# A new static order for a fused attention and mixture-of-experts kernel: due times, line counting and filler windows of its scheduler

## The chip, the core and the metric

The kernel runs on one core of a Trainium2 chip. A core has five engines, each with its own instruction stream: TensorE (PE in the profile; its weight loads are listed apart as PEld), VectorE (DVE), ScalarE (ACT), GpSimd (POOL) and SyncE (SP). Sixteen DMA engines move data between HBM and the on-chip memory, and all queues share them. The metric is the device time of one execution in microseconds. The median of the three runs of the kernel before is 178.59 us (177.97 to 179.07).

## The reference: banded attention, then soft mixture of experts

```python
# q, k, v: float32 [8 batches, 8 heads, 576 positions, 64]
scores = (q @ k.T) / sqrt(64)
# heads 0..3: position i sees i-31..i
# heads 4..7: position i sees every 4th of i-124..i
attn = softmax(where(mask[head], scores, -1e9)) @ v
x = attn.transpose(0, 2, 1, 3).reshape(4608, 512)

# phi [512, 32], w1 [8, 512, 1024], w2 [8, 1024, 512], float32
logits = x @ phi                          # [4608, 32]
d = softmax(logits, axis=0)               # over tokens
slot_input = (d.T @ x).reshape(8, 4, 512)
for e in range(8):
    slot_out[e] = relu(slot_input[e] @ w1[e]) @ w2[e]
out = softmax(logits, axis=1) @ slot_out.reshape(32, 512)   # [4608, 512]
```

The inputs are 61.9 MB in HBM, the output is 9.4 MB.

## The kernel before: units, stages, and a scheduler that writes the order

The attention is cut into eight **units**: a unit is a pair of batches and one of the two kinds of head (even units: plain band, odd units: dilated band). A unit arrives in one of three staging buffers `stg` as bf16 (the DMA converts), and goes through these stages, each a handful of PE instructions with its follow-up on another engine:

- **T** (`st_T`, four pieces; PE lines L582 for even and L577 for odd units): transposes of the staged rows into PSUM, copied into the buffer `TT` by ACT (L603). When the fourth piece has been transposed, the staging buffer is free for the load of the unit three later.
- **S** (`st_S`, six pieces; L621): scores, then exp on ACT (L628) into `PT`, then the mask on DVE (L636).
- **V** (`st_V`, four; L646): values transposed back, copied by DVE (L651) into `VN`.
- **P** (`st_P`, four; L675): probabilities times values, then a reciprocal and a product on DVE (L684, L686) into `XB`.
- **X** (`st_X`, four; L703): transposes of `XB`, copied to `XT` by DVE (L715) or ACT (L716), whichever the scheduler picks.
- **L, E, A** (`st_L`, for each batch after its odd unit; L730, L761, L774): logits and their exp, the exp transposed into `ET`, and the accumulation of slot inputs in PSUM.

After the last A come the closing stages, with due times from 1000 on: the folding of the accumulator (L861), the first expert product (L883), row sums (L930), transposes (L901), the second expert product `ffn2` (L957) as its weights arrive, then the output in two column halves for the first 1536 tokens (L1009, L1022; the factor `so_sb` of each half is made at L991) and whole for the rest (L1066). The weights `w1` go to the buffer `WD`; the last of `w2` go into `stg` (L806) and, for experts 5 to 7, into `TT` (L473), which only comes free when attention has read it.

All loads are issued by POOL in one fixed order (`load_first` L438, `load_unit` L417 and L424, `wload` L473, `wpair` L806), and each waits on POOL for its target buffer to come free. The stores are issued by SP and ACT.

No order is written by hand. Each instruction group is an `Op` with engine, cost and a **due time** (`key`). `Prog.schedule` is a greedy list scheduler that plays the program through with those costs: on each engine it looks for the earliest possible start, takes all ready groups that could start within 0.12 us of it, and places the one with the smallest due time. The order it finds is emitted as static streams with semaphores. Where the played-through PE would idle inside one of the windows of `FILL`, the scheduler inserts **fillers** (L1084): 512-column matmuls of a constant tile whose result nobody reads. Their number is fixed when the kernel is built; on the chip they are executed whether PE has the time or not.

Due times are `u * PACE + x`, with PACE = 13.1 for unit `u`, and an `x` for each stage: for example `0.5 * j` for T, `4.0 + 1.3 * i` for S, `8.5 + 2.0 * g` for P.

Of the kernel before, what the change touches and what calls it, by code (L numbers as in the profile page):

```python
# [16 lines left out]
N_SLOTS = 32  # L17
FF = 1024
SCALE = 1.0 / (D ** 0.5)
CT = 72  # L20
NU = 8
QB = 96
HALO = 32
FILL = ((1.5, 9.0, "h", 0.4, 0.43), (9.5, 13.5, "h", 0.6, 0.25), (13.5, 116.0, "h", 0.3, 0.216),
        (13.5, 24.0, "rf", 0.3, 0.216), (116.0, 143.0, "hrfc", 0.15, 0.216))


class DmaSem:
# [25 lines left out]
class Op:  # L54
    n = 0

    def __init__(self, e, fn, cost, key, mode):
        self.e, self.fn, self.cost, self.key, self.mode = e, fn, cost, key, mode
        self.deps, self.alloc, self.touch, self.sems = [], [], [], None
        self.end = self.ev = self.snap = None  # L60
        self.bytes = 0
        self.wr = []
        self.id = Op.n
        Op.n += 1
# [47 lines left out]
class Prog:  # L112
# [4 lines left out]
        self.ops = []  # L117

    def op(self, e, fn, r=(), w=(), a=(), alloc=(), cost=0.5, key=0.0, mode="f",
           sem=None, nbytes=0, after=(), ndma=1):  # L120
        o = Op(e, fn, cost, key, mode)
        deps = list(after)
        for b in r:
            deps += b.ready
        for b in w:
            b.fresh()
            deps += b.prev
        for b in a:
            deps += b.prev
        seen = set()  # L130
        for d in deps:
            if d.id not in seen:
# [12 lines left out]
        o.sems = sem  # L145
        o.bytes = nbytes
        o.ndma = ndma
        self.ops.append(o)
        return o

    def schedule(self, filler, fill_window):
# [13 lines left out]
        dma_free = 0.0  # L165
        mode = "f"
        order = []

        def place(o, t0, e):
            nonlocal dma_free, mode  # L170
            o.e = e
            cost = o.cost[e] if isinstance(o.cost, dict) else o.cost
            end = t0 + cost
            if e == "pe":
                if o.mode != mode:
                    end += 0.03
                mode = o.mode
            free[e] = end
            o.end = end
            if o.sems is not None:  # L180
                dma_free = max(dma_free, t0 + 3.2) + o.bytes / 424e3
                o.end = dma_free + 0.45
            for t in o.touch:
                t.left -= 1
                t.pool.use(t, o)
            order.append(o)

        while ready:
            picks = {}
            for o in ready:  # L190
                if o.e == "pool" and o is not pool_ops[ipool]:
                    continue
                if o.e == "sp" and o is not sp_ops[isp]:
                    continue
                got, tal, ok, taken = [], 0.0, True, {}
                for t in o.alloc:
                    f = t.pool.find(t.size, taken.get(id(t.pool), ()))
                    if f is None:
                        ok = False
                        break  # L200
                    got.append((t, f[0]))
                    tal = max(tal, f[1])
                    taken.setdefault(id(t.pool), []).extend(f[0])
                if not ok:
                    continue
                for e in (o.e if isinstance(o.e, tuple) else (o.e,)):
                    t0 = max(free[e], tal + self.LAT[e])
                    for d in o.deps:
                        t0 = max(t0, d.end + (self.LAT[d.e] if d.e != e or e != "pe" else 0.0))
                    if e == "pe" and o.mode != mode:  # L210
                        t0 += 0.08
                    picks.setdefault(e, []).append((t0, o, got))
            best = None
            for e, c in picks.items():
                lim = min(x[0] for x in c) + 0.12
                t0, o, got = min((x for x in c if x[0] <= lim), key=lambda x: (x[1].key, x[1].id))
                if best is None or t0 < best[0]:
                    best = (t0, o, got, e)
# [87 lines left out]
def bass_dilated_sliding_attn__then__soft_moe_slots_kernel(  # L306
# [93 lines left out]
    b_expT, b_expX = [Buf() for _ in range(B)], Buf()  # L400
    b_siT, b_h, b_hT, b_so = Buf(), [Buf(), Buf()], [Buf(), Buf()], [Buf(), Buf()]

    PACE = 13.1

    def due(u, x):
        return u * PACE + x

    def load_unit(u):
        bp, ty, s = u // 2, u % 2, u % 3
# [46 lines left out]
    def wload(name, parts=((0, 8, 0, 512),)):  # L456
        ap, b = HOME[name]
        e = int(name[2:])
        first_ = name[:2] == "w1"
        src = (moe_w1 if first_ else moe_w2)[e]  # L460
        c = 4 if first_ else 8
        v_ = src.rearrange("(p c) f -> p c f", c=c)
        d_ = ap.rearrange("p (c f) -> p c f", c=c)
        for lo, hi, c0, c1 in parts:
            if first_:
                dst, vs = d_, v_
            else:
                dst, vs = d_[:, lo:hi, c0:c1], v_[:, lo:hi, c0:c1]
            sem = DmaSem(nc, f"s_{name}_{len(b.parts)}")
            pb = Buf()  # L470
            for al in b.al:
                pb.prev = pb.prev + al.ready + al.reads
            o = op("pool", lambda g, dst=dst, vs=vs: [g.dma_start(dst, vs)],  # L473
                   after=pb.prev, a=[pb], cost=0.6, sem=sem,
                   nbytes=2097152 * (hi - lo) * (c1 - c0) // 4096)
            b.parts.append((lo, hi, c0, c1, pb))
            b.ready.append(o)

# [87 lines left out]
    def st_T(u, j):  # L566
# [5 lines left out]
        def pe(t):  # L572
            for a in range(2):
# [10 lines left out]
                            src[:, hx, c, :], ident[0:96, 0:96])  # L584
            return i_
        o = op("pe", pe, r=[b_id, b_stg[s] if u else b_half[j // 2]], w=[pt], alloc=[pt],
               cost=0.86 if ty == 0 else 0.75, mode="h" if ty == 0 else "f",
               key=due(u, 0.5 * j))
        if u == 0:
            b_stg[0].reads.append(o)  # L590

        def ev(ac):
# [9 lines left out]
                sv = sv.rearrange("p (s w) a k -> p s w a k", w=4)  # L602
            return ac.activation(d, sv, ACTF.Copy)  # L603
        op("act", ev, r=[pt], **{"w" if j == 0 else "a": [b_TT[u % 2]]}, cost=0.8,
           key=due(u, 0.8 + 0.5 * j))

    def bankb2(t, a):
        return psb[:, t.phys[0] + a, :]
# [1 line left out]
    def st_S(u, i):  # L610
# [4 lines left out]
        def pe(t):  # L615
# [7 lines left out]
                                  win(u, 0, h01, blk_, bpar)[64 * hx:64 * hx + 64],  # L623
                                  start=True, stop=True)
            return i_
        k0 = due(u, 4.0 + 1.3 * i)
        op("pe", pe, r=[b_TT[u % 2]], w=[sc], alloc=[sc, pt], cost=0.22, mode="r", key=k0)
        op("act", lambda ac: ac.activation(  # L628
            sbt(pt)[:, 0:768].rearrange("p (x n) -> p x n", x=2), pair(sc)[:, :, 0:384],
            ACTF.Exp, scale=SCALE), r=[sc], w=[pt], cost=0.71, key=k0 + 0.6)  # L630
# [2 lines left out]
        def mk(dv):  # L633
            m = mask[ty][:, m0:m0 + 4, :].rearrange("p m x -> p (m x)")
            p_ = sbt(pt)[:, 0:768].rearrange("p (x n) -> p x n", x=2)
            return dv.tensor_tensor(p_, p_, m.unsqueeze(1).to_broadcast([128, 2, 384]), AluOp.mult)  # L636
        op("dve", mk, r=[b_mask[ty]], w=[pt], cost=0.47, key=k0 + 1.5)

    def st_V(u, g):
        bpar, h01 = g // 2, g % 2  # L640
# [3 lines left out]
        def pe(t):  # L644
# [1 line left out]
                i_ = t.transpose(bankb(pv)[:, 128 * m:128 * m + 128],  # L646
                                 win(u, 2, h01, m, bpar), ident[:, :])
            return i_
        k0 = due(u, 4.5 + 2.0 * g)
        op("pe", pe, r=[b_id, b_TT[u % 2]], w=[pv], alloc=[pv, vn], cost=0.35, key=k0)  # L650
        op("dve", lambda dv: dv.tensor_copy(  # L651
            sbt(vn)[:, :, :, 0:64],
            bankb(pv)[:, 0:768].rearrange("p (m x d) -> p m x d", m=6, x=2)),
# [2 lines left out]
    def st_P(u, g):  # L656
# [12 lines left out]
        def pe(t):  # L669
# [6 lines left out]
                                  sbt(pts[i])[:, o_:o_ + 128],  # L676
                                  sbt(vn)[:, m, half, 0:65], start=True, stop=True)
            return i_
        k0 = due(u, 8.5 + 2.0 * g)
        op("pe", pe, r=list(pts.values()) + [vn], w=[po], alloc=al, cost=0.46, key=k0)  # L680

        def pv():
            return pair(po)[0:QB, :, 0:390].rearrange("p x (m d) -> p x m d", d=65)
# [7 lines left out]
    def st_X(u, bpar, x):  # L691
# [9 lines left out]
        def pe(t):  # L701
# [1 line left out]
                i_ = t.transpose(bankb(px)[:, QB * m:QB * m + QB],  # L703
                                 sbt(xb)[:, m, 128 * x:128 * x + 128], ident[0:QB, 0:QB])
            return i_
        k0 = due(u, 13.0 + 4.0 * bpar + 0.8 * x)
        op("pe", pe, r=[b_id, xb], w=[px], alloc=al, cost=0.31, key=k0)

        def ev(en):
            d, s_ = sbt(xt)[:, x, :], bankb(px)[:, 0:S]  # L710
# [9 lines left out]
    def st_L(b, u):  # L720
# [3 lines left out]
        def pe(t):  # L724
# [5 lines left out]
                    i_ = t.matmul(o_, phi_pad[:, c].rearrange("p j i -> p (j i)"), rhs,  # L730
                                  start=c == 0, stop=c == 3)
            return i_
        k0 = due(u, 15.5 + 4.0 * (b % 2))
        op("pe", pe, r=[x0, x1, b_phi], w=[lg], alloc=[lg], cost=1.0, key=k0)
# [4 lines left out]
        for h_ in range(2):  # L739
            def cp(dv, h_=h_):  # L740
                n = expT[:, S * b:S * b + S].rearrange("p (i y x) -> p x y i", x=2, y=2)
                return dv.tensor_copy(
                    expX[:].rearrange("p (x y i) -> p x y i", x=2, y=2)[:, :, h_],
                    n[:, :, h_, 96 * (1 - h_):96 * (1 - h_) + 48])
            op("dve", cp, r=[b_expT[b]], **{"w" if h_ == 0 else "a": [b_expX]}, cost=0.15,
               key=k0 + 2.2)
        pe_t = tile(psum, 1)
        et = tile(pET)

        def pe2(t):  # L750
# [13 lines left out]
        op("pe", pe2, r=[b_expT[b], b_expX, b_sel] + b_expT[b + 1:b + 2], w=[pe_t], alloc=[pe_t, et], cost=0.56, key=k0 + 2.4)  # L764
# [5 lines left out]
        def pe3(t):  # L770
# [8 lines left out]
        op("pe", pe3, r=[et, xb0, xb1], a=[b_acc, t_acc], cost=0.35, mode="c", key=k0 + 4.0)  # L779

    mk = sb("mk", [15, 5, 2, 4])
    turns = []
# [73 lines left out]
    for y in range(2):  # L856
        fo = tile(psum, 1)

        def pe_f(t, y=y, fo=fo):
# [4 lines left out]
        op("pe", pe_f, r=[b_psA, b_fold], w=[fo], alloc=[fo], cost=1.0, key=K1 - 0.5 + 0.1 * y)  # L864
# [214 lines left out]
    def filler(n):  # L1079
        t = tile(psum, 1)  # L1080

        def pe(te):
# [2 lines left out]
                               wrm[:].unsqueeze(1).to_broadcast([128, 4, 128]), start=True, stop=True)  # L1085
            return i_
        o = Op("pe", pe, 0.216 * n, -1, "f")
        t.left = 1
        o.touch = [t]
        o.alloc = [t]  # L1090
# [45 lines left out]
```

## Time and profile before

| | before |
|---|---|
| median of three runs | 178.59 us (177.97 to 179.07) |
| the profiled execution's own time | 177.96 us |
| its span on the core | 176.2 us |
| PE / DVE / ACT / POOL busy | 80% / 64% / 53% / 24% |
| HBM read / written | 61.93 MB / 9.44 MB |
| fillers (L1084) | 60 |

The busy shares are means over the whole span: PE's covers pipelined matmuls with modelled ends and the fillers. "DMA" in the 40 slices is the mean busy share of the 16 DMA engines in tenths, "GB/s" is what they wrote (for the loads half of what they read, since fp32 becomes bf16). The chain of waits is followed back from the last instruction, at each step to what released it. What lies around the span in the profiled execution is 177.96 - 176.2 = 1.8 us.

### The profile page before, as it was taken

Reading aid. Unit: us, or ns where it says so; the run is one execution under the profiler, and the core shown is the slowest. Engines: PE = TensorE matmul, PEld = TensorE weight load, DVE = VectorE, ACT = ScalarE, POOL = GpSimd, SP = SyncE. Lnnn points to the kernel's source line nnn. Section 1 sums busy time; section 2 is a strip of 40 time slices with the busy share of each in tenths; the row PEclk is TensorE's granted clock in tenths of the full one; section 3 lists DMA queues with packets and bytes.
Section 4 is the critical chain, followed back from the end, with each engine's and each line's share of the span. In section 5 each row is a group of like instructions: output and inputs, shape, how many; then the busy total and the mean of one; then the engine's idle time right before and its main releaser. Section 6 shows DMA issues by size and latency. Waiting matters only on the chain.

```text
span 176.2 us, 5741 instructions
## 1 busy us (share of the span) xinstructions
PE 140.8 (80%) x2573; PEld 100.2 (57%) x2574; DVE 113.5 (64%) x264; ACT 93.9 (53%) x143; POOL 42.3 (24%) x80
## 2 busy tenths in 40 slices
PE   7689988787988889797978898888999995599000
PEld 2166677566778667576956677864656643343000
DVE  6830986992897599479589489789932302379400
ACT  2044767744767875665875675774410201589300
POOL 7997105202200800500200200099900000000000
PEclk9969999999999999999999999999999999879955
DMA  4999999999999999999998999999999999999997
GB/s 70 176 238 202 197 217 210 229 230 192 215 215 212 228 230 193 216 209 217 237 219 190 216 219 214 216 214 219 214 205 206 208 194 196 305 326 398 450 424 298
DMA packets 12696, 40.80 MB, mean 232 GB/s; under 512 B 2240, under 2 KB 8896, under 8 KB 9408
## 3 DMA queue, kind: packets, MB, share of 16 engines
q0 software_dynamic: 8272, 30.94, 88.0%
q1 hardware_dynamic: 2768, 7.93, 11.4%
q10 hardware_dynamic: 1632, 1.57, 2.6%
q8 instruction: 20, 0.33, 0.7%
q14 instruction: 4, 0.03, 0.0%
HBM read 61.93 MB, written 9.44 MB: 405 GB/s over the span
## 4 chain that ended last, share of the span: by engine, by line
PE 33%; DVE 24%; DMA 18%; POOL 7%; ACT 6%; issue 4%; POOLq 0%; DVEq 0%
DMA TT<-in_moe_w_dram 15%; DVE PT L636 7%; DVE XB L686 7%; PE ps L582 7%; PE ps L577 5%; PE ps L703 4%; ACT PT L628 4%; DVE VN L651 4%; PE ps L730 4%; DVE WD L991 3%; DMA stg<-in_v_dram 3%; PE ps L646 3%; PE ps L621 3%; POOL TT L473 2%; POOL stg L806 2%
## 5 line engine op out<-in xcount | busy, mean ns | idle before, releaser
L603 ACT ACTIVATE TT<-ps 128x864 f32<-128x864 f32 x32 | 28.6, 896 | 27.6 <-PE ps L582 18.8
L628 ACT ACTIVATE PT<-ps 128x768 bf16<-128x768 f32 x48 | 36.7, 815 | 9.0 <-PE ps L621 8.9
L686 DVE TENSOR_TENSOR XB<-ps,RV 96x768 bf16<-96x768 f32 x32 | 30.3, 947 | 0.6
L651 DVE COPY VN<-ps 128x768 bf16<-128x768 bf16 x32 | 17.5, 546 | 6.3 <-PE ps L646 6.2
L1084 PE MATMUL ps<-wrm 128*128 128x512 bf16 x60 | 19.1, 446 | 1.1 <-DVE wrm L490 1.1
L675 PE MATMUL ps<-VN,PT 128*128 128x65 bf16 x384 | 17.8, 194 | 2.1 <-DVE PT L636 0.8
L582 PE MATMUL ps<-ident,stg 96*64 96x96 bf16 x576 | 16.0, 213 | 4.2 <-DMA stg<-in_v_dram 2.1
L715 DVE COPY XT<-ps 128x576 bf16<-128x576 bf16 x19 | 11.4, 598 | 10.9 <-PE ps L703 10.7
L582 PEld LDWEIGHTS ps<-ident,stg 96*64 96x64 bf16 x576 | 13.9, 114 | 7.5 <-DMA stg<-in_v_dram 2.6
L703 PE MATMUL ps<-ident,XB 96*128 96x96 bf16 x192 | 13.3, 207 | 4.9 <-DVE XB L686 3.3
L675 PEld LDWEIGHTS ps<-VN,PT 128*128 128x128 bf16 x384 | 14.5, 98 | 4.5 <-DVE PT L636 1.5
L992 ACT ACTIVATE WD<-ps,rtok 128x256 f32<-128x256 f32 (+1 forms) x22 | 10.7, 554 | 10.8 <-PE ps L1009 9.6
L646 PE MATMUL ps<-ident,TT 128*128 128x128 bf16 x192 | 16.0, 221 | 0.6 <-DVE VN L651 0.4
L621 PE MATMUL ps<-TT 64*128 64x96 bf16 x384 | 14.8, 204 | 1.2 <-ACT PT L628 1.1
L577 PE MATMUL ps<-ident,stg 96*128 96x96 bf16 x288 | 14.9, 206 | 0.3 <-DVE XB L686 0.3
L703 PEld LDWEIGHTS ps<-ident,XB 96*128 96x128 bf16 x192 | 9.6, 98 | 8.1 <-DVE XB L686 5.6
L636 DVE TENSOR_TENSOR PT<-PT,mask_d 128x768 bf16<-128x768 bf16 x24 | 12.9, 546 | 0.7 <-ACT PT L628 0.2
L577 PEld LDWEIGHTS ps<-ident,stg 96*128 96x128 bf16 x288 | 13.0, 98 | 0.4 <-DVE XB L686 0.4
L646 PEld LDWEIGHTS ps<-ident,TT 128*128 128x128 bf16 x192 | 10.8, 98 | 4.2 <-issue 1.3
L636 DVE TENSOR_TENSOR PT<-PT,mask_p 128x768 bf16<-128x768 bf16 x24 | 12.7, 539 | 0.1
L621 PEld LDWEIGHTS ps<-TT 64*128 64x128 bf16 x384 | 9.4, 94 | 5.8 <-ACT PT L628 2.5
L716 ACT ACTIVATE XT<-ps 128x576 bf16<-128x576 bf16 x13 | 8.5, 651 | 4.2 <-PE ps L703 3.9
(95 smaller groups left out, 184.1 us busy)
## 6 DMA issues: line engine op xcount, KB each, us to landing
WD<-in_moe_w_dram POOLq DMA_DIRECT2D x7, 1024.0 KB, 31.0
stg<-in_moe_w_dram POOLq DMA_DIRECT2D x5, 1024.0 KB, 25.7
stg<-in_q_dram POOLq DMA_DIRECT2D x4, 576.0 KB, 22.0
stg<-in_k_dram POOLq DMA_DIRECT2D x4, 576.0 KB, 24.0
stg<-in_v_dram POOLq DMA_DIRECT2D x4, 576.0 KB, 26.6
out_dram<-WD SPq DMA_DIRECT2D x2, 1024.0 KB, 5.3
out_dram<-WD SPq DMA_DIRECT2D x1, 2048.0 KB, 8.5
out_dram<-stg SPq DMA_DIRECT2D x1, 2048.0 KB, 10.8
```

Of the source, the lines that this page charges most:

```text
L577: i_ = t.transpose(bankb2(pt, a)[:, 96 * kk:96 * kk + 96], two[:, c, :], ident[0:96, 0:96])
L582: i_ = t.transpose(bankb2(pt, a)[64 * hx:64 * hx + 64, 96 * kk:96 * kk + 96], src[:, hx, c, :], ident[0:96, 0:96])
L603: return ac.activation(d, sv, ACTF.Copy)
L621: i_ = t.matmul(pair(sc)[:, hx, QB * x:QB * x + QB], win(u, 1, h01, blk_, bpar)[64 * hx:64 * hx + 64], win(u, 0, h01, blk_, bpar)[64 * hx: ...
L628: op("act", lambda ac: ac.activation(sbt(pt)[:, 0:768].rearrange("p (x n) -> p x n", x=2), pair(sc)[:, :, 0:384], ACTF.Exp, scale=SCALE), ...
L636: return dv.tensor_tensor(p_, p_, m.unsqueeze(1).to_broadcast([128, 2, 384]), AluOp.mult)
L646: i_ = t.transpose(bankb(pv)[:, 128 * m:128 * m + 128], win(u, 2, h01, m, bpar), ident[:, :])
L651: op("dve", lambda dv: dv.tensor_copy(sbt(vn)[:, :, :, 0:64], bankb(pv)[:, 0:768].rearrange("p (m x d) -> p m x d", m=6, x=2)), r=[pv], w= ...
L675: i_ = t.matmul(pair(po)[:, bk, 65 * po_:65 * po_ + 65], sbt(pts[i])[:, o_:o_ + 128], sbt(vn)[:, m, half, 0:65], start=True, stop=True)
L686: op("dve", lambda dv: dv.tensor_tensor(sbt(xb)[:].rearrange("p m (x h d) -> p h x m d", x=2, h=2)[:, h01], pv()[:, :, :, 0:64], sbt(rv)[: ...
L703: i_ = t.transpose(bankb(px)[:, QB * m:QB * m + QB], sbt(xb)[:, m, 128 * x:128 * x + 128], ident[0:QB, 0:QB])
L1084: i_ = te.matmul(bank(t).rearrange("p (a x) -> p a x", a=4), wrm[:], wrm[:].unsqueeze(1).to_broadcast([128, 4, 128]), start=True, stop=True)
```

## The change: other due times, a model of PE's instruction lines, a longer filler window

The diff, cut to its core:

```diff
+TOL, LINE, FETCH0 = 0.1297, 5.8, 193
+DUE = {"pace": 12.51, "T": -1.24, "Tj": 6.38, "Te": -39.52, "S": 10.02, "Si": 1.09,
+       "m": 13.16, "V": 10.46, "Vg": 5.39, "P": 9.84, "Pg": 7.23, "X": 43.57, "Xb": -45.81,
+       "L": 4.93, "Lb": -10.82, "x": 11.4}
...
-        (13.5, 24.0, "rf", 0.3, 0.216), (116.0, 143.0, "hrfc", 0.15, 0.216))
+        (13.5, 24.0, "rf", 0.3, 0.216), (116.0, 147.0, "hrfc", 0.15, 0.216))
...
+            if o.port and e in port:
+                port[e] = end
+            if e == "pe" and o.n:
+                done = 0
+                while count + o.n - done >= 256:
+                    done += 256 - count
+                    count = 0
+                    at = end - cost * (o.n - done) / o.n
+                    end += max(0.0, entry + LINE - at)
+                    entry = max(at, entry + LINE)
+                count += o.n - done
...
-                dma_free = max(dma_free, t0 + 3.2) + o.bytes / 424e3
+                dma_free = max(dma_free, t0 + 3.2) + o.bytes / 421.5e3
...
+                    if o.port and e in port:
+                        t0 = max(t0, port["pool" if e == "dve" else "dve"])
...
-                lim = min(x[0] for x in c) + 0.12
+                lim = min(x[0] for x in c) + TOL
...
-    PACE = 13.1
...
-        return u * PACE + x
+        return u * DUE["pace"] + x
...
-               key=due(u, 0.5 * j))
+               key=due(u, DUE["T"] + DUE["Tj"] * j))
...
-           key=due(u, 0.8 + 0.5 * j))
+           key=due(u, DUE["T"] + DUE["Te"] + DUE["Tj"] * j))
...
-        k0 = due(u, 8.5 + 2.0 * g)
+        k0 = due(u, DUE["P"] + DUE["Pg"] * g)
...
-        k0 = due(u, 13.0 + 4.0 * bpar + 0.8 * x)
+        k0 = due(u, DUE["X"] + DUE["Xb"] * bpar + 0.8 * x)
...
-        k0 = due(u, 15.5 + 4.0 * (b % 2))
+        k0 = due(u, DUE["L"] + DUE["Lb"] * (b % 2))
```

The scheduler's played-through PE now counts its instructions (two for each matmul). Each time the count passes 256, it enters a new line, and it may do so no earlier than 5.8 us after it entered the line before. S, V, the masks' key and the key of `expX` get new constants in the same way. The line `port` is without effect on the order: it is set for DVE groups alone, so the value that a DVE group compares with stays zero. Two costs of loads in the model change by a few per cent.

What this makes of the instruction streams: **POOL and SP keep their order, instruction for instruction**, and so do the groups of each engine after the last A, but for fillers. No DMA is added, removed or resized. Every group of the attention stays; what moves is:

- the interleaving on PE, DVE and ACT. For units 6 and 7, for example, with `T7.0` the first piece of T of unit 7 (fillers are `w`):

```
before  L4 X22 S6.0 V6.0 X23 S6.1 E4 L5 A4 V6.1 S6.2 S6.3 V6.2 E5 P6.0 S6.4 S6.5 A5
        V6.3 P6.1 P6.2 T7.0 X24 T7.1 X25 T7.2 P6.3 T7.3 X26 V7.0 S7.0 ...
after   X20 X21 V6.0 S6.0 V6.1 X22 X23 L4 S6.1 L5 E4 T7.0 P6.0 A4 E5 S6.2 S6.3 S6.4 A5
        V6.2 S6.5 P6.1 V6.3 T7.1 T7.2 P6.2 T7.3 P6.3 X24 X25 S7.0 V7.0 ...
```

- 12 of the 32 copies to `XT`, which go from DVE to ACT (19 and 13 before, 7 and 25 after);
- the fillers: 60 before, 75 after. Ahead of the first S 26 in both; from there to the last A 25 before and 9 after; behind the last A 9 before and 40 after:

```
before  A7 w*4 fold F1 row sums transposes w*5  ffn2*64                  half 0 ffn2*14 half 1 rest
after   A7 w*4 fold F1 row sums transposes w*11 ffn2*32 w*19 ffn2*24 w*2 ffn2*4 w*4 ffn2*4
        half 0 ffn2*14 half 1 rest
```

More of the change, by code (lines that the diff above doesn't have):

```diff
@@ L61, in __init__ @@
         self.bytes = 0
+        self.n = 0
+        self.port = False
         self.wr = []
@@ L119, in op @@
     def op(self, e, fn, r=(), w=(), a=(), alloc=(), cost=0.5, key=0.0, mode="f",
-           sem=None, nbytes=0, after=(), ndma=1):
+           sem=None, nbytes=0, after=(), ndma=1, n=0, port=False):
         o = Op(e, fn, cost, key, mode)
@@ L147, in op @@
         o.ndma = ndma
+        o.n = 2 * n
+        o.port = port
         self.ops.append(o)
@@ L167, in schedule @@
         order = []
+        count, entry = 256 - FETCH0, -LINE
+        port = {"dve": 0.0, "pool": 0.0}
         def place(o, t0, e):
-            nonlocal dma_free, mode
+            nonlocal dma_free, mode, count, entry
             o.e = e
@@ L474, in wload @@
                    after=pb.prev, a=[pb], cost=0.6, sem=sem,
-                   nbytes=2097152 * (hi - lo) * (c1 - c0) // 4096)
+                   nbytes=2097152 * (hi - lo) * (c1 - c0) * (108 if c1 - c0 < 512 else 100) // 409600)
             b.parts.append((lo, hi, c0, c1, pb))
@@ L586, in st_T @@
         o = op("pe", pe, r=[b_id, b_stg[s] if u else b_half[j // 2]], w=[pt], alloc=[pt],
-               cost=0.86 if ty == 0 else 0.75, mode="h" if ty == 0 else "f",
-               key=due(u, 0.5 * j))
+               cost=0.86 if ty == 0 else 0.75, mode="h" if ty == 0 else "f", n=18 if ty else 36,
+               key=due(u, DUE["T"] + DUE["Tj"] * j))
         if u == 0:
@@ L625, in pe @@
             return i_
-        k0 = due(u, 4.0 + 1.3 * i)
-        op("pe", pe, r=[b_TT[u % 2]], w=[sc], alloc=[sc, pt], cost=0.22, mode="r", key=k0)
+        k0 = due(u, DUE["S"] + DUE["Si"] * i)
+        op("pe", pe, r=[b_TT[u % 2]], w=[sc], alloc=[sc, pt], cost=0.22, mode="r", n=8, key=k0)
         op("act", lambda ac: ac.activation(
@@ L636, in mk @@
             return dv.tensor_tensor(p_, p_, m.unsqueeze(1).to_broadcast([128, 2, 384]), AluOp.mult)
-        op("dve", mk, r=[b_mask[ty]], w=[pt], cost=0.47, key=k0 + 1.5)
+        op("dve", mk, r=[b_mask[ty]], w=[pt], cost=0.47, key=k0 + DUE["m"], port=True)
     def st_V(u, g):
@@ L648, in pe @@
             return i_
-        k0 = due(u, 4.5 + 2.0 * g)
-        op("pe", pe, r=[b_id, b_TT[u % 2]], w=[pv], alloc=[pv, vn], cost=0.35, key=k0)
+        k0 = due(u, DUE["V"] + DUE["Vg"] * g)
+        op("pe", pe, r=[b_id, b_TT[u % 2]], w=[pv], alloc=[pv, vn], cost=0.35, n=6, key=k0)
         op("dve", lambda dv: dv.tensor_copy(
@@ L678, in pe @@
             return i_
-        k0 = due(u, 8.5 + 2.0 * g)
-        op("pe", pe, r=list(pts.values()) + [vn], w=[po], alloc=al, cost=0.46, key=k0)
+        k0 = due(u, DUE["P"] + DUE["Pg"] * g)
+        op("pe", pe, r=list(pts.values()) + [vn], w=[po], alloc=al, cost=0.46, n=12, key=k0)
         def pv():
@@ L705, in pe @@
             return i_
-        k0 = due(u, 13.0 + 4.0 * bpar + 0.8 * x)
-        op("pe", pe, r=[b_id, xb], w=[px], alloc=al, cost=0.31, key=k0)
+        k0 = due(u, DUE["X"] + DUE["Xb"] * bpar + 0.8 * x)
+        op("pe", pe, r=[b_id, xb], w=[px], alloc=al, cost=0.31, n=6, key=k0)
         def ev(en):
@@ L732, in pe @@
             return i_
-        k0 = due(u, 15.5 + 4.0 * (b % 2))
-        op("pe", pe, r=[x0, x1, b_phi], w=[lg], alloc=[lg], cost=1.0, key=k0)
+        k0 = due(u, DUE["L"] + DUE["Lb"] * (b % 2))
+        op("pe", pe, r=[x0, x1, b_phi], w=[lg], alloc=[lg], cost=1.0, n=8, key=k0)
         op("act", lambda ac: ac.activation(
@@ L745, in st_L @@
             op("dve", cp, r=[b_expT[b]], **{"w" if h_ == 0 else "a": [b_expX]}, cost=0.15,
-               key=k0 + 2.2)
+               key=k0 + DUE["x"], port=True)
         pe_t = tile(psum, 1)
@@ L763, in pe2 @@
             return i_
-        op("pe", pe2, r=[b_expT[b], b_expX, b_sel] + b_expT[b + 1:b + 2], w=[pe_t], alloc=[pe_t, et], cost=0.56, key=k0 + 2.4)
+        op("pe", pe2, r=[b_expT[b], b_expX, b_sel] + b_expT[b + 1:b + 2], w=[pe_t], alloc=[pe_t, et], cost=0.56, n=12, key=k0 + 2.4)
         op("dve", lambda dv: dv.tensor_copy(
@@ L778, in pe3 @@
             return i_
-        op("pe", pe3, r=[et, xb0, xb1], a=[b_acc, t_acc], cost=0.35, mode="c", key=k0 + 4.0)
+        op("pe", pe3, r=[et, xb0, xb1], a=[b_acc, t_acc], cost=0.35, n=12, mode="c", key=k0 + 4.0)
     mk = sb("mk", [15, 5, 2, 4])
@@ L863, in pe_f @@
             return i_
-        op("pe", pe_f, r=[b_psA, b_fold], w=[fo], alloc=[fo], cost=1.0, key=K1 - 0.5 + 0.1 * y)
+        op("pe", pe_f, r=[b_psA, b_fold], w=[fo], alloc=[fo], cost=1.0, n=4, key=K1 - 0.5 + 0.1 * y)
         for hi in range(2):
@@ L1087, in filler @@
         o = Op("pe", pe, 0.216 * n, -1, "f")
+        o.n = 2 * n
         t.left = 1
```

## The prediction, made before the changed kernel was run

> **What bounds the kernel.** I read the 40 slices first, because they tell at once whether any resource is full from end to end.
>
> ```profile
> span 176.2 us, 5741 instructions
> ...
> DMA  4999999999999999999998999999999999999997
> GB/s 70 176 238 202 197 217 210 229 230 192 215 215 212 228 230 193 216 209 217 237 219 190 216 219 214 216 214 219 214 205 206 208 194 196 305 326 398 450 424 298
> ...
> q8 instruction: 20, 0.33, 0.7%
> ...
> HBM read 61.93 MB, written 9.44 MB: 405 GB/s over the span
> ```
>
> The reader should see that no slice of the DMA row but the first and last is below 8. PE shows 80% and DVE 64%, both with holes; the 16 DMA engines have none. The packets of the trace say it more sharply: from 4 us to the end of the stores, the time that engines stand without a packet adds up to 0.59 us in units of all sixteen; 0.30 of it lies between 154 and 156, and some 0.1 at the very end. The loads run from about 4.2 to 152.4 us: 61.93 MB in 148.2 us, 418 GB/s. Then stores alone run to 176.2.
>
> Next the chain of waits, which seems to say something else (PE 33%, DVE 24%, DMA 18%). Its pieces in order of time (start us, us, what):
>
> ```profile
> 47.08 0.44 PE ps L774 x12
> ...
> 75.88 0.44 PE ps L774 x12
> ...
> 104.12 0.44 PE ps L774 x12
> ...
> 121.72 3.45 POOL TT L473 x5
> ...
> 126.60 25.85 DMA TT<-in_moe_w_dram
> 152.49 0.32 PE ps L957 x4
> ```
>
> The chain goes back from the last weight to the moment when POOL issued it (126.60), and from there through attention. But the 25.85 us are not a transfer of 256 KB: they are a queue that was never empty. So the attention part of the chain is not what sets the end, unless the queue runs dry. How far it is from that: POOL's waits for a staging buffer are long (columns: us in total, times, longest us),
>
> ```profile
> POOL stg L424 <- PE ps L577: 22.7, 2, 12.7
> POOL stg L417 <- PE ps L582: 21.6, 3, 11.3
> ```
>
> and yet the first load issued behind such a wait lands 18 to 28 us after its issue (22.1 us for the 576 KB issued at 43.07; 18.3 us for the 1 MB at 114.92), of which its own transfer is some 3 to 5 us. At least 13 us of queue stand before it each time.
>
> Last, what PE waits for when the last weights come in (start, us, engine, line, shapes, idle time before and its releaser):
>
> ```profile
> 146.45 0.29 PE L957 MATMUL ps<-TT,hT 128*32 128x256 bf16 x4 [0.55 <-DMA TT<-in_moe_w_dram]
> 147.74 0.29 PE L957 MATMUL ps<-TT,hT 128*32 128x256 bf16 x4 [1.00 <-DMA TT<-in_moe_w_dram]
> ...
> 151.07 0.29 PE L957 MATMUL ps<-TT,hT 128*32 128x256 bf16 x4 [0.20 <-DMA TT<-in_moe_w_dram]
> 152.49 0.29 PE L957 MATMUL ps<-TT,hT 128*32 128x256 bf16 x4 [1.12 <-DMA TT<-in_moe_w_dram]
> ```
>
> PE is there first, but narrowly: 0.55 + 1.00 = 1.55 us ahead of half 0, another 0.20 + 1.12 = 1.32 ahead of half 1. This is the slack of the whole compute side: 1.55 us before half 0 moves, 2.87 before half 1 moves. Behind half 1 the DMA engines have only half 0's stores to work on, so half 1's lateness is paid one for one.
>
> **The change, part by part.** *DMA*: the same transfers in the same order on POOL and SP, and the staging buffers are freed by the same pieces of T. To starve the queue they would have to be freed 13 us later; T of a unit moves by a few groups. Cost 0; if that cover were gone, one for one.
>
> *Fillers behind the last A*: 31 more. Rows of L1084 give 0.38 us for one and 1.04 for four, so (1.04 - 0.38)/3 = 0.22 us each, and 31 x 0.22 = 6.8 us in front of the last weights' matmuls. They cost nothing only as far as PE would have waited there: half 0 is late by 6.8 - 1.55 - E = 5.25 - E, half 1 by 6.8 - 2.87 - E = 3.9 - E, where **E** is by how much attention ends earlier (last A at 131.8 to 132.3 before). All hangs on E.
>
> *E, the new interleaving*. Before, from A to A of a batch pair takes 75.88 - 47.08 = 28.8 and 104.12 - 75.88 = 28.2 us. Three floors lie below. The loads: unit 3's values land at 17.2 + 27.1 = 44.3, unit 7's at 71.6 + 26.1 = 97.7, so 53.4/2 = 26.7 us for a pair. PE's lines: a pair has 568 matmuls, 1136 instructions, 4.44 lines of 256; the instruction queue's packets (20 of 16 KB) start 5.86 to 6.1 us apart where PE is densest and 6.29 on average from the fifth to the seventeenth, so 26.0 to 27.1 us. The engines: DVE is busy 22.1 and ACT 19.7 us in the pair from 44.5 to 73.2; moving three XT copies for each pair (598 ns on DVE, 651 on ACT) makes that about 20.3 and 21.6, so DVE, which led most of the waiting stretches of the chain, gets easier and ACT does not become the bound. PE's 24.9 us include the two fillers. I expect 27.2 us: that is 28.5 - 27.2 = 1.3 a pair, 2.6 for two. The stretch up to 47.1 is bound below by unit 3's landing at 44.3, so it can give 0 to 2.8; I take 1.0, because its first units already wait for loads. The last stretch, 104.1 to 132.3, has the same work, no loads to wait for and 7 fillers less, of which most were in idle time: 0.7. So E = 2.6 + 1.0 + 0.7 = **4.3 us**. The ends: 0 (the new order does no better than the old), and 6.4 (two pairs at 26.7, 3.6 us, and 2.8 of the start).
>
> With 4.3, half 0 is 0.95 us late and half 1 is not (3.9 - 4.3 < 0). Half 0's lateness costs nothing: the loads, which until 152.4 share the DMA engines with its stores, go ahead by as much, and its 1.57 MB still cover the gap until half 1's stores. An E of 6 gains nothing either, since the weights do not come sooner.
>
> *Line counting against a rule.* The trace shows PE idle for nothing visible at such places, for example 1.65 us at 40.86 and 0.75 at 59.30 (L582 and L703, releaser "issue"). [...]
>
> *Clock*: the granted clock is 0.82 in the rows of 150 to 155 and 155 to 160, after PE's thinnest stretch (2.85 us busy of 145 to 150). With fillers there it may stay at 1.0, and the output matmuls (2.34 us for ten against 1.26 in half 0) get shorter. What this can return is bounded by the 0.30 us of idle DMA engines there; I take 0.1.
>
> **Sum**: 0 (DMA) + 0 (half 1 hidden) - 0.1 (clock): 177.9 on the profiled execution's 177.96. The median shown is 0.63 above that, so **178.4** beside 178.59: no change.
>
> **Rivals.** *The fillers are paid* (slower): the place is behind the last A, the price 3.9 - E on the end, it decides from E < 3.9, that is when the last A comes after 128.4. For: E has three terms, each a reading of a margin, and a scheduler that plays costs places fillers by its own clock, not the chip's; in the chain two fillers at 38.27 already stood before late work. At E = 2 the end moves 1.9 us (180.3), at E = 0.5 by 3.4 (181.8); below E = 2.1 it is over 1%. Chance of that 0.22.
>
> *The line counting describes nothing*: then the stalls that are called "issue" stay where they are and pairs keep 28.5 us; only start and end give (1.7), half 1 is late by 2.2, and the median 180.7. This is contained in the first as its cause; I give it 0.06 more.
>
> *The chain is right and attention sets the end* (faster): then E comes off the whole, 174.3. Against it stand the full DMA row and the 18 to 28 us of queue. Or the same bytes move faster when instruction fetches and stores fall differently: slices of the loads range from 190 to 238 GB/s, but as large packets end unevenly, and 1% would need 1.8 us where 0.59 are idle. Together 0.08.
>
> **How the numbers follow.** About 1% (1.8 us) is what a measurement of this kernel can tell from no change. No change 0.64 by the sum; slower 0.22 + 0.06 = 0.28; faster 0.08. The range takes the forecast's spread (177.3 from all idle DMA time, a little below for the runs' own 0.6%) and E down to about 1.5: 176.9 to 181.0, which leaves out the far end of either rival. The forecast's own range is 177.3 to 179.6.
>
> **What would show it.** Right: the DMA row unbroken up to the stores, the last load landing at 152 to 153, the last A (L774 of before) at 127 to 129, PE waiting for `TT` at the last `ffn2` of half 1, fillers before it, a span of 175.7 to 176.7. Wrong: PE arriving at those matmuls after the weights (no wait for DMA, the releaser PE itself), a dip of the DMA row at 151 to 156, or the last A near 132. If the last load itself lands clearly before 151 with the same bytes, the rate was not fixed, and my whole reading of the bound fails.

## The result: slower by 1.5%, by fillers that ran ahead of the last weights' matmuls

| | before | changed |
|---|---|---|
| median | 178.28 us (177.85 to 179.07, 4 runs) | 181.06 us (180.54 to 181.40, 4 runs) |
| span of the profiled execution | 176.2 us | 179.7 us |
| ratio | 1 | 1.0148, 95% interval 1.0101 to 1.0196 |
| last A starts | 131.83 us | 131.14 us |
| `so_sb` of half 0, of half 1 | 148.09, 152.84 us | 152.02, 155.07 us |
| first store of output on the DMA engines | 150.36 us | 154.23 us |
| DMA engines without a packet, 4 us to the end | 0.58 us | 3.86 us |

The last row is the time during which engines have no packet, as a share of all sixteen, added up from the trace's DMA packets. Its growth, 3.28 us, is nearly the growth of the span, 3.5 us.

The 40 slices of the changed kernel's page (granted PE clock, busy share of the DMA engines, and what they wrote):

```profile
span 179.7 us, 5790 instructions
...
PEclk9969999999999969999995699996999999999955
DMA  5999999999999999999999999999999998599996
GB/s 74 171 229 219 199 217 210 243 197 208 215 217 215 231 222 191 218 213 211 235 213 199 215 219 217 210 221 215 212 208 221 186 196 116 192 342 397 418 460 292
```

The DMA row, in which only the first and the last slice were below 8 before, now has an 8 and a 5 at its 34th and 35th digit (from 148 to 157 us), with 116 GB/s in the first. That is the dip which the prediction named as the sign of the slower case. The same place in windows of 3 us, first of the kernel before, then of the changed one (busy us and number of instructions of PE, PEld, DVE, ACT and POOL, then granted clock, DMA share, GB/s):

```profile
150.00:153.00 3.00, 1.46 (x16) 0.70 (x14) 0.95 (x3) 1.83 (x5) 0.00 (x0) 1.00 1.15 286
153.00:156.00 3.00, 2.62 (x12) 1.83 (x14) 1.77 (x4) 1.88 (x5) 0.00 (x0) 0.54 0.94 321
```

```profile
150.00:153.00 3.00, 2.41 (x20) 0.97 (x19) 0.49 (x2) 0.12 (x1) 0.00 (x0) 1.00 0.42 55
153.00:156.00 3.00, 2.41 (x28) 1.74 (x26) 2.20 (x4) 2.37 (x7) 0.00 (x0) 1.00 0.45 150
```

And what PE does ahead of it, from the changed kernel's instructions in order of time (start, us, engine, line, shapes; L1105 are the fillers, L978 is `ffn2`, L1012 makes `so_sb`):

```profile
142.06 1.91 PE L978 MATMUL ps<-stg,hT 128*32 128x512 bf16 x32
143.90 4.28 PE L1105 MATMUL ps<-wrm 128*128 128x512 bf16 x19
...
149.94 0.61 PE L1105 MATMUL ps<-wrm 128*128 128x512 bf16 x2
150.48 0.29 PE L978 MATMUL ps<-TT,hT 128*32 128x256 bf16 x4
150.70 1.04 PE L1105 MATMUL ps<-wrm 128*128 128x512 bf16 x4
151.67 0.29 PE L978 MATMUL ps<-TT,hT 128*32 128x256 bf16 x4
152.02 0.48 DVE L1012 TENSOR_SCALAR so_sb<-ps,rcs 128x256 bf16<-128x256 f32 x1 [11.81 <-PE ps L978]
```

None of these matmuls waits for a DMA any more. Before, the two groups of four that close half 0 had waited 0.55 and 1.00 us for weights; now the weights lie there, and PE works through fillers that hide nothing.

### The profile page after: what moved, and what is told of

It reads as the page before. It is cut to its first block, busy times and chain, and to the rows that moved or that the text cites. A ratio compares the mean times of both kernels' runs of the same rounds, so it can differ in the third digit from the quotient of the medians.

```text
span 179.7 us, 5790 instructions
## 1 busy us (share of the span) xinstructions
PE 145.6 (81%) x2589; PEld 105.6 (59%) x2589; DVE 108.3 (60%) x252; ACT 98.1 (55%) x155; POOL 42.2 (24%) x80
## 3 DMA queue, kind: packets, MB, share of 16 engines
q1 hardware_dynamic: 2768, 7.93, 11.2%
## 4 chain that ended last, share of the span: by engine, by line
PE 45%; ACT 13%; DVE 12%; DMA 10%; POOL 7%; issue 6%; ACTq 1%; POOLq 0%
DMA stg<-in_v_dram 10%; ACT WD L1013 6%; PE ps L1105 6%; PE ps L603 6%; PE ps L751 5%; PE ps L696 4%; PE ps L724 4%; DVE XB L707 4%; DVE PT L657 4%; ACT PT L649 4%; PE ps L667 3%; POOL stg L459 3%; PE ps L782 3%; PE ps L642 3%; PE ps L598 3%
## 5 line engine op out<-in xcount | busy, mean ns | idle before, releaser
L624 ACT ACTIVATE TT<-ps 128x864 f32<-128x864 f32 x32 | 27.9, 896 | 25.2 <-PE ps L603 20.5
L603 PE MATMUL ps<-ident,stg 96*64 96x96 bf16 x576 | 17.7, 225 | 8.6 <-issue 5.5
L1105 PE MATMUL ps<-wrm 128*128 128x512 bf16 x75 | 21.7, 434 | 1.1 <-DVE wrm L511 1.1
L603 PEld LDWEIGHTS ps<-ident,stg 96*64 96x64 bf16 x576 | 15.7, 124 | 10.7 <-issue 6.5
L737 ACT ACTIVATE XT<-ps 128x576 bf16<-128x576 bf16 x25 | 15.4, 656 | 3.5 <-PE ps L724 3.5
L667 PE MATMUL ps<-ident,TT 128*128 128x128 bf16 x192 | 16.7, 226 | 0.4 <-DVE VN L672 0.4
L705 DVE RECIPROCAL RV<-ps 96x12 f32<-96x12 f32 x32 | 7.2, 224 | 12.3 <-PE ps L696 12.2
L1105 PEld LDWEIGHTS ps<-wrm 128*128 128x128 bf16 x75 | 7.4, 110 | 11.1 <-issue 5.4
L667 PEld LDWEIGHTS ps<-ident,TT 128*128 128x128 bf16 x192 | 11.6, 101 | 3.0 <-issue 0.6
L724 PE MATMUL ps<-ident,XB 96*128 96x96 bf16 x192 | 12.7, 220 | 0.4 <-DVE XB L707 0.3
```

Source lines behind the costliest of these rows:

```text
L603: i_ = t.transpose(bankb2(pt, a)[64 * hx:64 * hx + 64, 96 * kk:96 * kk + 96], src[:, hx, c, :], ident[0:96, 0:96])
L667: i_ = t.transpose(bankb(pv)[:, 128 * m:128 * m + 128], win(u, 2, h01, m, bpar), ident[:, :])
L724: i_ = t.transpose(bankb(px)[:, QB * m:QB * m + QB], sbt(xb)[:, m, 128 * x:128 * x + 128], ident[0:QB, 0:QB])
L1105: i_ = te.matmul(bank(t).rearrange("p (a x) -> p a x", a=4), wrm[:], wrm[:].unsqueeze(1).to_broadcast([128, 4, 128]), start=True, stop=True)
```

## The experiments: what was paid, and why attention came no earlier

Theory 1 says that the 31 additional fillers behind the last A make the loss. Theory 2 says why they were not hidden: attention could not end earlier, because PE's instructions come in lines of 256 no faster than about one in 6 us (in the changed kernel's trace the 16 KB packets of the instruction queue start 5.80 us apart at the least and 6.46 on average from the fifth to the seventeenth). The rivals are that the new interleaving or its DMA timing costs something itself, and that the engines' waits for each other set attention's pace. Ratios are against the kernel before on the same chip; the other columns are read from one profiled execution of each.

| kernel | last A, us | `so_sb` half 0, us | first store, us | DMA idle, us | ratio (95%) |
|---|---|---|---|---|---|
| changed | 131.1 | 152.0 | 154.2 | 3.9 | 1.0148 (1.0101 to 1.0196) |
| e1: few fillers | 132.3 | 147.7 | 150.3 | 0.7 | 0.9991 (0.9969 to 1.0013) |
| e2: before + 31 | 133.0 | 153.9 | 156.1 | 5.5 | 1.0287 (1.0225 to 1.0348) |
| e3: 16 ahead of half 1 | 130.3 | 148.6 | 150.9 | 3.4 | 1.0085 (1.0053 to 1.0117) |
| e4: short T | 124.8 | 147.9 | 150.3 | 0.5 | 0.9975 (0.9959 to 0.9991) |
| e5: short T, padded | 127.5 | 148.3 | 150.6 | 0.4 | 0.9984 (0.9963 to 1.0006) |
| e6: half 0 late | 133.5 | 153.1 | 155.4 | 5.2 | 1.0270 (1.0245 to 1.0296) |
| e7: no counting | 133.2 | 148.3 | 150.5 | 0.4 | 0.9995 (0.9976 to 1.0013) |
| e8: four blocks in halves | 132.3 | 148.6 | 150.8 | 2.4 | 1.0037 (1.0020 to 1.0055) |

The kernel before, e2, e3, e6 and e8 run attention in one and the same order on PE, and their last A lies between 130.3 and 133.5 us. So a difference of less than some 3 us in the first column shows nothing by itself.

### e1: the changed order with the old number of closing fillers

```diff
+CAP = {1002.0: 5, 1003.0: 0, 1011.0: 0, 1012.0: 0, 1021.0: 0}   # due time of the group behind the filler
...
-                n = min(int((t0 - ts - slack) / each + 0.05), 64)
+                n = min(int((t0 - ts - slack) / each + 0.05), CAP.get(o.key, 64))
```

> The changed order of every engine, but behind the last A only the 9 fillers of the kernel before (4 and 5) instead of 40. Theory 1 (the loss is the 31 fillers in front of the last weights' matmuls): PE waits for the last weights again, half 0's so_sb comes at 148 us instead of 152.0, the DMA engines' idle time falls from 3.9 us to under 1, and the time is that of the kernel before: ratio 0.997 to 1.003. Rival (the new interleaving or its DMA timing costs something itself): the ratio stays at 1.010 or more.

The loss is gone: 0.9991, with every attention group in the changed order. PE waits for the last weights as it did in the kernel before (PE in order of time, idle time before and its releaser in brackets):

```profile
146.02 0.29 PE L981 MATMUL ps<-TT,hT 128*32 128x256 bf16 x4 [0.50 <-DMA TT<-in_moe_w_dram]
147.36 0.29 PE L981 MATMUL ps<-TT,hT 128*32 128x256 bf16 x4 [1.05 <-DMA TT<-in_moe_w_dram]
```

So the new interleaving costs nothing by itself. No gain shows either: the last A is at 132.3, within the spread of the kernel before.

### e2: the kernel before with the 31 fillers

```diff
+FORCE = {1002.0: 6, 1003.0: 19, 1011.0: 2, 1012.0: 4}
...
+            if e == "pe" and FORCE.get(o.key):
+                x = filler(FORCE.pop(o.key))
+                ...
+                place(x, max(free["pe"], f[1] + 0.1), "pe")
```

> The kernel before, instruction for instruction, with the 31 fillers added where the changed kernel has them (6, 19, 2 and 4). Theory 1: half 0 is late by 31 x 0.22 - 1.55, about 4.6 to 5.2 us (0.7 more than in the changed kernel, whose last A was 0.7 us earlier), and the span grows by about 4 us, ratio 1.020 to 1.026. Rival (fillers there are free, the order costs): ratio 1.000 to 1.005.

1.0287 (1.0225 to 1.0348), past the upper end of what was expected: the last A also came 1.2 us later in its profiled execution, so that half 0 was 5.8 us late. Its slices show the changed kernel's dip, but deeper, 4 and 5 where that has 8 and 5:

```profile
DMA  5999999999999999999999999999999994599996
GB/s 76 168 224 212 207 213 214 234 215 199 214 211 216 235 219 193 216 213 218 230 207 212 209 224 209 222 209 222 208 200 208 195 199 54 179 339 391 418 458 292
```

With e1 this shows theory 1 from both sides: the fillers make the loss on either order, and neither order has it without them.

### e3 and e6: which half's lateness is paid

e3 delays half 1 alone, by 16 fillers ahead of its `ffn2`:

```diff
+FORCE = {1030.0: 16}
```

> The kernel before with 16 fillers (3.5 us) put between half 0 and half 1's ffn2: half 0 is not touched, half 1 is late by 3.5 - 1.32 = 2.2 us, as it was in the changed kernel (2.23). If half 1's lateness alone is what is paid, the span grows by 2.2 us (ratio 1.012), and the changed kernel's 3.5 us of span have 1.3 unexplained. If half 0's lateness counts more (the DMA engines stand idle between the end of the loads and half 0's first store), half 0's stores cover part of this gap here and the span grows by clearly less than the changed kernel's, 1 to 2.2 us.

e6 delays half 0 without a filler, by putting its output matmuls behind half 1's `ffn2`, which waits for the last weights:

```diff
-    mm0 = half(0, K1 + 20)
-    ffn2([(6, cc) for cc in range(2, 8)], 1, K1 + 30, after=mm0)
+    ffn2([(6, cc) for cc in range(2, 8)], 1, K1 + 30)
...
+    half(0, K1 + 20, behind=chain[-1:])
     half(1, K1 + 40)
```

(`behind` is new: it makes the output matmuls of a half wait for the group that it names, here the last `ffn2` of half 1.)

> The kernel before with half 0's output matmuls put behind half 1's ffn2, so they wait for the last weights: half 0's first store comes some 4.5 us later (150.4 before), while half 1's so_sb stays at 152.8 to 153 and its matmuls come 1.3 us later, behind half 0's. No filler is added. If half 0's lateness is what is paid (the DMA engines have nothing between the end of the loads, about 151.2 without competing stores, and the first store), the engines stand idle 3 to 3.7 us and the ratio is 1.015 to 1.02. If only half 1's lateness is paid, as the prediction had it, the span grows by 0 to 1.3 us, ratio 1.000 to 1.007.

e3 cost 1.0085, 1.5 us: half 1's lateness is paid, though less than the 2.2 us by which it was to be late. (The profiled execution of e3 took 181.07 us beside a median of 179.33; half 1 was 3.5 us late in it, with PE at a granted clock of 0.70 at 150 to 153 us, so its row of the table shows more idle time than can be usual for it.) e6 cost far more, 1.0270 and more than the 1.015 to 1.02 expected, though no filler was added and the two `so_sb` were started at 153.1 and 153.5. Half 0's first store came 5.1 us late in it instead of 4.5, with the last A at 133.5. Its windows, and the group that half 0 waits behind:

```profile
150.00:153.00 3.00, 1.24 (x13) 0.41 (x10) 0.00 (x0) 0.00 (x0) 0.00 (x0) 0.68 0.43 58
153.00:156.00 3.00, 2.40 (x16) 1.68 (x13) 2.06 (x5) 1.75 (x4) 0.00 (x0) 0.50 0.15 50
```

```profile
152.64 0.40 PE L957 MATMUL ps<-TT,hT 128*32 128x256 bf16 x4 [1.25 <-DMA TT<-in_moe_w_dram]
```

The last packet of the loads ends at 152.1 to 152.3 us in these kernels, and from there to half 0's first store the DMA engines have nothing. In three kernels the arithmetic is nearly the same: first store less the idle time gained over the kernel before is 154.23 - 3.28 = 150.95 in the changed kernel, 156.10 - 4.95 = 151.15 in e2, 155.42 - 4.65 = 150.77 in e6. The kernel before has its first store at 150.36. So in these three half 0 is late by some 0.4 to 0.8 us for nothing, and what lies beyond is paid. In the changed kernel this accounts for nearly the whole span: ahead of its first store the idle time grew from 0.10 to 3.18 us, behind it only from 0.48 to 0.68, so half 1's 2.23 us added 0.2 at most.

### e4 and e5: is it PE's time or PE's instructions that sets attention's pace?

e4 takes instructions away in the even units' T:

```diff
-                    for hx in range(2):
-                        i_ = t.transpose(
-                            bankb2(pt, a)[64 * hx:64 * hx + 64, 96 * kk:96 * kk + 96],
-                            src[:, hx, c, :], ident[0:96, 0:96])
+                    i_ = t.transpose(bankb2(pt, a)[:, 96 * kk:96 * kk + 96],
+                                     two[:, 36 * a + 9 * j + kk, :], ident[0:96, 0:96])
```

> The changed order with all its fillers, but the transposes of the even units' T are made by 18 instructions of 128 columns for each piece, as in odd units, instead of 36 of 64; what they transpose is laid out otherwise, so this stage computes a different arrangement of the same data. PE's own time falls by about 0.1 us a piece (0.89 to 0.77 us), 0.5 us a pair, but PE's instructions fall by 144 a pair, 0.56 of a line of 256. Theory 2 (attention gained only 0.7 us because PE's lines come no faster than one in 6.0 to 6.5 us): the last A comes 3 us or more earlier than in the changed kernel (at 128 or before, 131.1 there), the fillers are then hidden and the ratio falls to 1.000 to 1.005. Rival (the engines' mutual waits set the pace): the last A at 129.5 to 130.5, ratio 1.007 to 1.012.

e5 gives PE the time back, and more, in few instructions:

```diff
         def pe(t):
+            for a in range(0 if ty else 2):
+                t.matmul(ps[:, pt.phys[0] + a, :].rearrange("p (a x) -> p a x", a=4), wrm[:],
+                         wrm[:].unsqueeze(1).to_broadcast([128, 4, 128]), start=True, stop=True)
```

> As the run before with short T (18 instructions of 128 columns a piece in even units, another arrangement of the same data), but each such piece begins with two 512-column matmuls of a constant into its own banks, 0.22 us each. A piece then takes PE about 0.77 + 0.43 = 1.2 us instead of 0.89 in the changed kernel: PE has 1.2 us more to do in a pair than there, but 128 instructions fewer (20 matmuls a piece for 36). Theory 2 (lines of instructions set attention's pace): the last A stays near 125 to 127.5 and the ratio at 0.996 to 1.003. Rival (it was PE's time that the short T saved): the last A is at 131 us or later and the ratio 1.012 or more.

Neither e4 nor e5 gives the kernel's output, since both leave out the arrangement of the data that the next stages expect; they tell what sets the pace and are no versions to use. With 144 instructions fewer a pair the last A came at 124.8, 6.3 us before the changed kernel's; all 40 closing fillers were still there, and the time was 0.9975 of the kernel before, a little below what was expected. With PE's time in T padded above the changed kernel's, the last A was still at 127.5 and the ratio 0.9984. Last A of e4, then of e5:

```profile
124.80 0.70 PE L793 MATMUL ps<-XB,ET 96*32 96x256 bf16 x12 [0.16 <-DVE ET L784]
```

```profile
127.46 0.51 PE L796 MATMUL ps<-XB,ET 96*32 96x256 bf16 x12 [0.15 <-DVE ET L787]
```

In e4 attention runs into the loads, as the chain of waits on its page says (shares of the span by engine; DMA had 10% in the changed kernel):

```profile
DMA 56%; PE 16%; POOL 9%; ACT 8%; DVE 2%; issue 2%; ACTq 1%; POOLq 0%
```

From the first A to the last, where the start of the kernel does not enter, e4 takes 79.1 and e5 79.2 us; the changed kernel takes 85.3, e1 with the same order 83.8, and the kernel before 84.8. In this stretch PE is busy for 69.6 us in e4 and 72.5 in e5: 2.9 us more of PE's work cost nothing, and the number of instructions is what made the difference. (PE was busy for 74.7 us there in the changed kernel, some of them at half clock.) Nearly all of the 2.7 us between their last As were there at the first A already (45.7 and 48.3). So theory 2 holds as far as it says "instructions, not PE's time". What PE's weight loads waited for "issue" fell with it, from 11.2 us in the changed kernel (13.9 in e1) to 5.8 and 6.2. One more thing differed that was not held fixed: PE ran at half its clock for 13.7 us between first and last A in the changed kernel, 10 in e1, and 3.4 in e4 and in e5. How the 5 to 6 us that were won divide between shorter stalls and the higher clock is not shown.

That attention 7 us earlier than before returns only 0.25% also shows once more that it is not what sets the end.

### e7: the same due times with the line counting off

```diff
-TOL, LINE, FETCH0 = 0.1297, 5.8, 193
+TOL, LINE, FETCH0 = 0.1297, 0.0, 193
```

(and e1's `CAP`)

> The changed kernel's due times with the scheduler's line counting off (5.8 us set to 0), and the closing fillers of the kernel before (4 and 5). It shows what the counting does to the order. Theory 2: the lines come as fast as the queue delivers them whatever the model believes, so the last A lies between 130 and 134 as in the changed order with few fillers (132.3), the stalls called issue lie elsewhere, and the ratio is 0.996 to 1.003. Rival (the counting makes the order better on the chip): the last A is later than 135, and if it passes 135 by more than a microsecond the time grows too.

Last A at 133.2 beside e1's 132.3, ratio 0.9995 beside 0.9991. On these due times, what the model knows of the lines does not show in the time. Whether it helps attention stays open: the last As differ by less than executions of one order do, though from the first A to the last this one execution takes 87.4 us where those with the counting take 83.8 and 85.3.

### e8: less of the output in halves

```diff
-    NAB = 6
-    GRP = [2] * NAB + [4, 4, 8, 8]
+    NAB = 4
+    GRP = [2] * NAB + [4, 4, 4, 8, 8]
...
-    for i, (n, hs) in enumerate(((4, (3,)), (4, (4,)), (8, (5, 6)), (8, (7, 8)))):
+    for i, (n, hs) in enumerate(((4, (2,)), (4, (3,)), (4, (4,)), (8, (5, 6)), (8, (7, 8)))):
```

> The kernel before with the first 1024 tokens instead of the first 1536 stored in column halves (1 KB rows), and one more group of four tokens a partition stored whole. Theory (DMA sets the end): 1.05 MB move from packets of 1 KB (45.6 ns each, 16 engines: 359 GB/s) to larger ones (about 430 GB/s), 0.5 us less; but half 0's stores, 1.05 MB and 2.9 us of the engines, may not reach from the end of the loads to half 1's first store, so 0 to 0.5 us come back: ratio 0.996 to 1.000. Rival (the stores of half 0 must be as many as now): ratio 1.003 or more.

This was tried as a version that might beat both. It is slower, 1.0037, as its rival said: in the windows of its profiled execution (179.50 us beside a median of 178.86) the DMA engines run out between half 0 and half 1.

```profile
153.00:156.00 3.00, 2.28 (x12) 1.44 (x14) 1.48 (x3) 1.40 (x4) 0.00 (x0) 0.50 0.70 235
```

Half 0's stores are the bridge from the loads to half 1; a third of them less cost 0.7 us here. (The granted clock was 0.50 from 150 to 156 us in this execution; what part that had in the gap was not tried.)

## Why the prediction was wrong

**The bound was right.** The loads end at 152.1 us in both kernels, no staging buffer came too late, and e4 shows that even 7 us of attention shorten the kernel by only 0.25%. The forecast of "no gain" rested on this, and so did the place and the sign of the rival that came true. Its price was near by luck: 3.9 - E is half 1's lateness, 3.2 us at E = 0.7, where the span grew by 3.5; but half 1 was 2.2 us late, and half 0's lateness is what was paid.

**The term that failed first is E**, put at 4.3 us, and in it the 27.2 us for a batch pair, down from 28.5. E measured 0.7 in the changed kernel's profile and -0.4 in e1. With last As that differ by 3 us in one and the same order, this says that E is near 0 and not 4.3, and no more. From the chain of the changed kernel (start us, us, what; L795 is A):

```profile
45.94 0.44 PE ps L795 x12
...
61.41 2.78 issue
64.19 1.91 PE ps L603 x48
...
76.50 0.44 PE ps L795 x12
...
93.78 1.73 issue
...
105.84 0.44 PE ps L795 x12
```

The pairs take 76.50 - 45.94 = 30.6 and 105.84 - 76.50 = 29.3 us, longer than the 28.8 and 28.2 before. The start gave 1.1 us and the last stretch 2.4 (forecast 1.0 and 0.7); the two pairs, which were to give 2.6, took back 2.9; and 0.7 is left. In the five profiles with the old order a pair takes 27.2 to 29.6 us, 28.3 on average; in the two with the new order 28.4 to 30.6, 29.6 on average. What PE's weight loads waited for between 20 and 132 us, the longest of the kernel before (us in total, times, longest us):

```profile
PEld ps L703 <- DVE XB L686: 5.6, 9, 0.7
PEld ps L774 <- DVE ET L765: 3.8, 7, 0.8
...
PEld ps L582 <- issue: 1.7, 1, 1.7
```

and of the changed one:

```profile
PEld ps L603 <- issue: 6.1, 4, 2.9
PEld ps L642 <- issue: 2.3, 6, 0.9
PEld ps L696 <- DVE PT L657: 1.9, 2, 1.4
...
PEld ps L724 <- DVE XB L707: 0.8, 3, 0.4
```

The new order did what the forecast expected of it: DVE's `XB` no longer holds PE up, 5.6 us before and 0.8 for the same wait after. But the time did not go to the end. Part of it became a new wait whose long pieces fall where PE enters a new line (the last section has the counts): all rows called "issue" add up to 7.2 us before and 11.2 after (5.5 to 8.8 in the other profiles of the old order, 13.9 in e1). Part of it is no wait at all: all rows of the two views together fell, from 27 to 24 us, and yet attention ended hardly earlier, because PE worked more slowly. Two of the windows of the changed kernel in which the granted clock fell (the column before the last two):

```profile
65.00:70.00 5.00, 4.91 (x108) 4.27 (x104) 2.37 (x5) 3.19 (x5) 1.44 (x3) 0.71 0.94 198
95.00:100.00 5.00, 4.50 (x71) 4.04 (x72) 1.74 (x3) 2.41 (x4) 1.06 (x2) 0.52 0.98 205
```

The trace has the clock at one half from 64.5 to 67.9, from 95.2 to 102.0 and from 122.5 to 125.9 us; between 15 and 150 us the profile of the kernel before has it nowhere. In these 13.7 us the transposes of T start 39 ns apart instead of 21 and the matmuls of P 54 instead of 33; over all stages that makes some 4.9 us, an estimate from these distances. The forecast had no term for it. No run kept the clock up on this order, so how much of E each of the two took stays open.

On the instructions, the forecast had named the floor of 26.0 to 27.1 us that PE's lines set, and then placed its own number 0.1 us above the upper end, as if the lines could be used without a gap. The floor itself left out the average that the forecast quotes beside it: 4.44 lines at 6.29 us make 27.9 us, more than the 27.2 expected. A floor made from the shortest distances between packets of the instruction queue (5.86 to 6.1 us) is not a pace; in the changed kernel the same packets came 6.46 us apart on average, no faster than before. The longest stall of the changed kernel shows how a line is late: PE enters a line at about 56.5 us and is through with its 256 instructions (126 matmul records and their weight loads) at 61.4, in the T of an even unit (72 instructions in 0.89 us); the next packet, 7.65 us behind the one before it, runs from 61.9 to 62.8, and PE goes on at 64.2. Where the long stalls fall differs from one execution to the next: e1, with the same order, has its longest at 36.9 and 69.6 us.

**The second step that failed** is "half 0's lateness costs nothing". The forecast let the loads go ahead by as much as half 0's stores were late. They did not: their last packet ended at 152.13 us beside 152.09 before, although no store competed with them. At 150.5 us, just behind half 0's first store in the kernel before, the loads had 0.11 MB left to write there and 0.09 in the changed kernel, half a microsecond at the 0.20 MB per us at which they came from 148 to 149. So there was next to nothing that could go ahead, and then nothing is left to move. e6 shows it without fillers. By the forecast's own formula, with E = 0.7, half 0 is late by 4.55 and half 1 by 3.2 us; they were late by 3.9 and 2.2. With half 1 as the only price the changed kernel would have lost 2.2 us of span; it lost 3.5.

**The fillers' price** was right, 0.22 us each: 19 of them took 4.28 us and five of the kernel before 1.24. What the formula had too low is the slack ahead of them. The 24 `ffn2` matmuls ahead of its last two groups took 2.7 us before (143.19 to 145.9), where their weight loads waited 0.20 and 0.48 us for a DMA, and 1.8 in the changed kernel (148.11 to 149.94). This is about the 0.6 us by which half 0, and most of the 1.0 by which half 1, was less late than the formula gives.

**The clock** behind attention came back as foreseen, granted 1.00 between 150 and 156 us where it had fallen to 0.54 from 153 on. It returned nothing that can be seen beside the idle DMA engines.

**The second rival**, that the line counting describes nothing, does not hold. Of the sixteen crossings into the next line of 256 instructions between 19 and 116 us in the changed kernel ten show no stall, but six stop PE for 0.53 to 2.78 us, 7.4 in all, and attention ends earlier when it has fewer instructions (e4 at 124.8 and e5 at 127.5 us, beside 131.1). This rival gave 180.7 us, close to the 181.06 measured, and half 1 was late by the 2.2 us that it named; but this is luck, since half 0's lateness was paid and the stalls did not stay where they were, they grew.

Two small slips in the forecast change nothing: its sum gives 178.5 us where it writes 178.4, and the granted clock of 155 to 160 us, quoted as 0.82, is 0.83 in its row.

Among the rivals, the one that came true had 0.22, with a point of decision at E < 3.9. The range ended at 181.0, just short of the 181.06 measured, because E below 1.5 was left out, though 0 had been written down as the end of its bounds.

## What to carry to other kernels

A filler is only as cheap as the wait that it was meant for. If its number is fixed from played-through times, then a stage that is late by a few microseconds turns each of them into delay; put them where the slack has been measured, and count the slack from the trace. When one resource is full from end to end, look for the places where it changes from one supply to the next, here from loads to stores: the work that bridges them had half a microsecond of slack, though it seemed to be hidden. And where an order is made denser, count its instructions beside its times.

## What the runs showed of the hardware that was not expected

- PE stood for up to 2.9 us (its weight load at 64.19 us) where it goes from one line of 256 instructions into the next. The six stalls called "issue" on the changed kernel's chain between 37 and 96 us end at the 605th, 859th, 1112th, 1240th, 1620th and 1748th matmul record, that is 254, 253, 128, 380 and 128 apart: within a few records (some are missing from a trace) multiples of 128 matmuls, 256 instructions with their weight loads. In the kernel before such stalls end at the 605th, 988th, 1243rd, 1625th and 1753rd record, 383, 255, 382 and 128 apart. The instruction queue has 20 packets of 16 KB beside 5178 matmuls and weight loads in the changed kernel, 259 for each. Its next packet starts 2.7 to 5.4 us after PE has entered a line there, and its packets start no less than 5.80 us apart there and 5.86 in the kernel before.
- Close to such stalls the granted clock fell: 0.71 in the window of 65 to 70 us and 0.52 in that of 95 to 100 of the changed kernel, just behind the stalls that end at 64.19 and 95.50, but it was also at one half from 122.5 to 125.9, with no such stall near; the profile of the kernel before has 1.00 from 15 to 150 us, with stalls of up to 1.5 us. That the lower clock follows from the stall was not tried.
- In attention, PE with fewer instructions and more time of work for each T (e5, 1.2 us a piece by the lengths of its parts, where the changed kernel has 0.89) took 79.2 us from the first A to the last, the changed order with more instructions 83.8 and 85.3.
